# Attention, MLP and top-1 experts on one core: the expert memory taken from attention's rings, six of 13 late token slots turned by TensorE

## The chip, the cores and the metric

One core of a Trainium2 chip runs the whole program. The metric is the device time of one execution in microseconds (us), as the median of several runs. Engines are named as in the profile: PE is TensorE (PEld its weight loads), DVE is VectorE, ACT is ScalarE, POOL is GpSimd, SP is SyncE, which here only issues transfers. A tile pool with n buffers under one tag is called a ring: the n-th next user of the tag waits until the buffer's readers are done.

## The reference

Four batches of 8 heads, head width 64, with 512 local and 32 global tokens. Attention, then a plain MLP, then a mixture of eight experts of which each token takes one:

```python
s_ll = where(|i - j| <= 32, scale * q_l @ k_l.T, -1e9)       # local, window 32
a_l  = softmax(concat([scale * q_l @ k_g.T, s_ll]))
out  = concat([softmax(scale * q_g @ k_all.T) @ v_all, a_l @ v_all])
x    = out.reshape(2304, 512)
h    = x @ w_in                                              # 512 -> 2048
x    = (h * sigmoid(h)) @ w_out                              # 2048 -> 512
e    = argmax(x @ w_gate); p = softmax(x @ w_gate)[e]
out  = p * sigmoid(x @ w_output_gate)[e] * (relu(x @ w1[e]) @ w2[e])   # 512 -> 1024 -> 512
```

## The kernel before

Matrix products are made from 16-bit halves: each f32 operand is scaled by a power of two and split into a high and a low f16, and three products (high by high, high by low, low by high) are summed in PSUM. Batch 0's attention is in f32, so it can start on raw inputs.

**Start.** SP issues the loads in the order of the code (L1407 to L1417): q of tile 0, all of k of batch 0, cs (mask columns), q of tile 1, cr (a table of constants with the identity for PE's transposes), the first 1 MB of w_in, v of batch 0, and the rest. `scale_v0` (L315) squares v on ACT (L319), sums over partitions on PE (L192, `tot`) and derives the power-of-two scale of batch 0's v; then attention steps run: scores on PE (L475), softmax (L454), transposes of the probabilities on PE (L489, L490), products with v (L497, L498). DVE rebuilds f32 from the 64-bit w_in (L381 to L383). The instruction order on each engine is set by a scheduler that runs over the program before the launch; priorities (`tc.high_priority`, with URG = 2000 the most urgent) and `tc.issue_after` bend it.

**Middle.** The other attention steps are interleaved with the MLP: h products (L681), SiLU on ACT and DVE (L683 to L701), x products (L728). Each 128-token tile of x is split into halves x2s, which go to x2d in DRAM (L752, 512 columns high and 512 low).

**Routing.** x2f is turned on PE (x2t, L766) for the gate (L776). From one-hots come each token's rank in its expert and from that a slot of 128 tokens: 8 early slots, one per expert, filled from the first 15 tiles, and 23 others, of which 13 are worked on here ("late" slots). A product of A (position one-hots) with Rc or RE (slot one-hots) gives the row numbers: `pme` (L1124) and from it `idge` (L1125) for the early slots, `pm` (L1173) and from it `idg` (L1174) for the late ones. `pce` and `pcf` give the gate coefficients in the same way, `pt` the output rows.

**Experts.** Slot n's tokens are gathered from x2d by an indirect DMA on POOL (xg, L1241) and transposed by a DMA that SP issues (x, L1243). `mm_h` multiplies by a quarter (256 columns) of w1 (hp, L1286 or L1278 and L1281), makes relu and the halves on ACT and DVE (r, hb; L1299 to L1306), and has hb of two slots transposed by another DMA of SP (L1313). `mm_y` multiplies by the matching rows of w2 (yp, L1323) and adds into ys. Four such quarters ("chunks") run; weights come as 512 KB loads into the ring `ws` (L918) and are split by ACT (L954) and DVE (L955). w1 and w2 of chunk 0 are there before routing ends. The early slots run first, the late ones after `last()` (L1141), which makes idg. The buffers of the late part (`ys`, which also holds the gathered xg; `xs` for transposed x; `r` with three buffers for r and two for hb; six for ws) lie in pools that are opened when the routing's and the MLP's pools are closed:

```python
        rt_ctx.close()
        mlp_ctx.close()

        ys_p = ctx.enter_context(tc.tile_pool(name="ys", bufs=1))
        xs_p = ctx.enter_context(tc.tile_pool(name="xs", bufs=1))
        r_p = ctx.enter_context(tc.tile_pool(name="r", bufs=3))
        moe.pools = (xs_p, r_p, ys_p)
        wm["s"], wm["n"] = ctx.enter_context(tc.tile_pool(name="ws", bufs=6, side="right")), 3
```

Until then ws has two buffers. `rest` (L1352) then issues, in this order, the late gathers, chunk 0's coefficients and, behind the last late transpose, the loads of w1's next chunk.

Of the kernel before, what the change touches and what calls it, by code (L numbers as in the profile page):

```python
# [9 lines left out]
F32 = mybir.dt.float32  # L10
# [42 lines left out]
NEARLY = NE  # L53
ORDER = (*range(14), 16, 14, 15)
# [52 lines left out]
def tile_kernel(ctx: ExitStack, tc, csa, csr, q0, q, qn, qg, k0, k, va, vc, w_in, w_out, wg, w1, w2, out, dbg=None):  # L107
# [11 lines left out]
    g_p = mlp_ctx.enter_context(tc.tile_pool(name="g", bufs=6))  # L119
    gt_p = mlp_ctx.enter_context(tc.tile_pool(name="gt", bufs=2))  # L120
    x2_p = mlp_ctx.enter_context(tc.tile_pool(name="x2", bufs=2))
# [75 lines left out]
    woh = wto.tile([128, KF, DM], F16, name="woh")  # L197
    wol = wto.tile([128, KF, DM], F16, name="wol")
# [68 lines left out]
    def load_k0():  # L267
        kt[0] = k_p.tile([128, 4, S], F32, tag="k", name="k0")
        SP.dma_start(kt[0], k0)
# [35 lines left out]
    def load_v0():  # L305
        vt[0] = v_p.tile([128, 5, DM], F32, tag="v", name="v0")
        SP.dma_start(vt[0][:, 0:4], va[0])
        SP.dma_start(vt[0][0:SG, 4], vc[0])
# [136 lines left out]
    pt, av, sums, xs = {}, {}, {}, {}  # L445

# [5 lines left out]
    ident = cr[:, C_ID:C_ID + 128]  # L452

# [13 lines left out]
    def att0_s(t, pr):  # L467
# [4 lines left out]
        for hh in range(2):  # L472
            p, h = divmod(2 * pr + hh, 4)
            p = slice(64 * p, 64 * p + 64)
            PE.matmul(ps[:, hh, 0:wl], qt[t][p, h], kt[0][p, h, 128 * t:128 * t + wl])  # L475
            if t:
                PE.matmul(ps[:, hh, wl:wt], qt[t][p, h], kt[0][p, h, 0:SG])
        e = e_p.tile([128, 2, 256], F32, tag="e", name="e")
# [502 lines left out]
    def route(rt, rps):  # L981
# [9 lines left out]
        DVE.tensor_scalar(trib, iota, cr[:, C_P:C_P + 1], None, ALU.is_gt)  # L991
        ones = T([128, 128], "ones", BF16)
# [14 lines left out]
        Rc = T([128, NT, 3, NSLOT], "Rc", BF16)  # L1007
        Rce = Rc.rearrange("p i c n -> p (i c n)")[:, 0:45 * NEARLY].rearrange("p (i c n) -> p i c n", c=3, n=NEARLY)
        RE = Rce[:, :, 2]
# [26 lines left out]
        apend, pc_i = [], [None]  # L1036
# [55 lines left out]
        def early(i):  # L1092
# [11 lines left out]
            else:  # L1104
# [3 lines left out]
                coef(14, 15)  # L1108

                DVE.tensor_scalar(n0[:, 1], n0[:, 1], 128.0, None, ALU.max)  # L1110
                r, SR = slice(0, 15), [128, 15, NE]
                DVE.tensor_scalar(u[:, r, 0], dhi[:, r], 0.0, None, ALU.is_equal)
                DVE.tensor_tensor(RE, ohf[:, r], bc(u[:, r], SR), ALU.mult)
                static(0, 15)

        def early_slots():
            pump_a(99)
            SR = [128, 15, NEARLY]
            for c in range(2):
                DVE.tensor_tensor(Rce[:, :, c], RE, bc(row[c][:, 0:15], SR), ALU.mult)  # L1120
            pm = rps.tile([128, NEARLY], F32, tag="av", name="pme")
            for i in range(15):
                for c in range(2):
                    PE.matmul(pm, A[:, i], Rce[:, i, c], start=(i == 0 and c == 0), stop=(i == 14 and c == 1))  # L1124
            DVE.tensor_scalar(idge, pm, -1.0, 0.0, ALU.add, ALU.max)  # L1125
# [15 lines left out]
        def last():  # L1141
            p = onehot(15, 17)
            DVE.tensor_tensor(n0[:, 2], n0[:, 1], p[:, 0, 0], ALU.add)
            n1 = T([128, NE, 1], "n1")
            DVE.tensor_tensor(n1[:, :, 0], n0[:, 2], p[:, 0, 1], ALU.add)
            cmp = d.rearrange("p i e -> p (i e)").rearrange("p (e i) -> p e i", e=NE)
            S3t = [128, NE, NT]
            DVE.tensor_tensor(cmp, bc(n1, S3t), bc(cr[:, C_CNT:C_CNT + NT].rearrange("p (a i) -> p a i", a=1), S3t), ALU.is_gt)
            sl = T([128, NE], "sl")
            DVE.tensor_reduce(sl, cmp, AX.X, ALU.add)  # L1150
            DVE.tensor_scalar(sl, sl, -float(NS), 0.0, ALU.add, ALU.max)
            DVE.tensor_tensor_scan(bnd[:, 0], one8, sl, 0.0, ALU.mult, ALU.add)
            base = T([128, 1, NE], "base")
            DVE.scalar_tensor_tensor(base[:, 0], bnd[:, 0], float(ST - NS), sl, ALU.add, ALU.subtract)
            ranks(15, 17, p, n0[:, 1:3])
            static(15, 17)
            S3 = [128, NT, NE]
            DVE.tensor_tensor(tmp, ohf, bc(base, S3), ALU.mult)
            b_ = T([128, NT, 1], "b_")
            DVE.tensor_reduce(b_[:, :, 0], tmp, AX.X, ALU.add)  # L1160
            DVE.tensor_tensor(b_[:, :, 0], b_[:, :, 0], u[:, :, 0], ALU.mult)
            DVE.tensor_tensor(b_[:, :, 0], b_[:, :, 0], dhi, ALU.add)
            SR = [128, NT, NSLOT]
            R = Rc[:, :, 2]
            i24 = iota[:, 0:NSLOT].rearrange("p (a n) -> p a n", a=1)
            DVE.tensor_tensor(R, bc(i24, SR), bc(b_, SR), ALU.is_equal)
            for c in range(2):
                DVE.tensor_tensor(Rc[:, :, c], R, bc(row[c], SR), ALU.mult)
            pump_a(99)
            pm = rps.tile([128, NSLOT], F32, tag="av", name="pm")  # L1170
# [42 lines left out]
    class Moe:  # L1213
# [138 lines left out]
        def rest(self, ny, wq):  # L1352
            ne, ns = self.ne, self.ns
            self.experts()
            while wpend or wq:
                pump_w(wq)
# [233 lines left out]
```

## Time and profile before

| what | us |
|---|---|
| median of 3 runs (lowest, highest) | 865.5 (864.69, 870.08) |
| the profiled execution | 872.73 |
| span of its trace | 870.9 |
| mean granted TensorE clock | 0.964 of full speed |

The profile is of one execution. Its rows give the start in us from the span's beginning, the duration of a group of like instructions, engine, line, operation, output tile from input tiles, and in brackets how long the engine had stood idle before and what released it. Busy times per stretch are given per engine with the number of instructions; PEclk is the granted clock as a share of full speed, DMA the mean busy share of the core's 16 DMA engines.

### The profile page before, as it was taken

Reading aid. Unit: us, or ns where it says so; the run is one execution under the profiler, and the core shown is the slowest. Engines: PE = TensorE matmul, PEld = TensorE weight load, DVE = VectorE, ACT = ScalarE, POOL = GpSimd, SP = SyncE. Lnnn points to the kernel's source line nnn. Section 1 sums busy time; section 2 is a strip of 40 time slices with the busy share of each in tenths; the row PEclk is TensorE's granted clock in tenths of the full one; section 3 lists DMA queues with packets and bytes.
Section 4 is the critical chain, followed back from the end, with each engine's and each line's share of the span. In section 5 each row is a group of like instructions: output and inputs, shape, how many; then the busy total and the mean of one; then the engine's idle time right before and its main releaser. Section 6 shows DMA issues by size and latency. Waiting matters only on the chain.

```text
span 870.9 us, 17387 instructions
## 1 busy us (share of the span) xinstructions
PE 769.5 (88%) x6201; PEld 525.3 (60%) x6201; DVE 590.1 (68%) x1649; ACT 516.8 (59%) x1017; POOL 58.1 (7%) x110
## 2 busy tenths in 40 slices
PE   2999969899899999999999889968759998899894
PEld 2898656566666766677666557545425655455541
DVE  2978876777767878767565556872126787588862
ACT  2685768677667667666545555411359846756710
POOL 0000000000000000000000000035000000000054
PEclk9999888999999999999999999979979999999997
DMA  9733444366974284646354262199975974885672
GB/s 356 292 121 123 150 149 161 107 145 167 183 122 89 48 176 99 137 86 122 67 99 106 95 146 65 46 194 194 197 202 174 237 143 151 181 167 170 141 175 90
DMA packets 182139, 127.83 MB, mean 147 GB/s; under 512 B 161437, under 2 KB 162973, under 8 KB 178592
## 3 DMA queue, kind: packets, MB, share of 16 engines
q1 hardware_dynamic: 178688, 116.67, 55.5%
q0 software_dynamic: 3360, 9.97, 3.9%
q8 instruction: 54, 0.88, 0.4%
q14 instruction: 37, 0.30, 0.1%
HBM read 76.93 MB, written 9.96 MB: 100 GB/s over the span
## 4 chain that ended last, share of the span: by engine, by line
PE 42%; DMA 20%; DVE 14%; issue 9%; ACT 9%; SPq 2%; POOL 1%; POOLq 0%; ACTq 0%; DVEq 0%
PE h L681 10%; PE x L728 10%; DMA ws<-in_w_dram 6%; PE yp L1323 5%; DMA pT<-pb 4%; DMA wil<-hb 4%; PE hp L1286 3%; PE av L531 2%; PE s L475 2%; DMA st<-in_qn_dram 2%; DVE w1b L955 2%; DVE k L210 2%; PE av L497 1%; PE av L498 1%; ACT w1b L954 1%
## 5 line engine op out<-in xcount | busy, mean ns | idle before, releaser
L728 PE MATMUL x<-woh,g 128*128 128x512 f16 x544 | 173.5, 381 | 0.3 <-ACT g L711 0.3
L681 PE MATMUL h<-xT,wih 128*128 128x256 f16 (+1 forms) x1152 | 162.0, 272 | 3.6 <-DMA xT<-xb 1.5
L681 PEld LDWEIGHTS <-wih 128*128 128x128 f16 x1152 | 109.3, 100 | 29.5 <-issue 4.7
L728 PEld LDWEIGHTS <-g 128*128 128x128 f16 x816 | 76.3, 98 | 80.4 <-issue 2.6
L1323 PE MATMUL yp<-w2b,wil 128*128 (+1 forms) x384 | 93.4, 390 | 19.5 <-DMA wil<-hb 11.9
L728 PE MATMUL x<-wol,g 128*128 128x512 f16 x272 | 103.8, 382 | 0.0
L1286 PE MATMUL hp<-w1b,x 128*128 128x256 f16 (+1 forms) x672 | 87.8, 279 | 8.9 <-DMA x<-xg 4.7
L681 PE MATMUL h<-xT,wil 128*128 128x256 f16 (+1 forms) x576 | 87.3, 273 | 0.0
L1286 PEld LDWEIGHTS <-x 128*128 128x128 f16 x672 | 67.0, 101 | 27.6 <-issue 5.9
L464 ACT ACTIVATE e<-e,mx,esc 128x192 f32<-128x192 f32 (+1 forms) x128 | 70.5, 553 | 19.1 <-DVE mx L461 17.5
L228 ACT ACTIVATE junk<-ws 128x1024 f16<-128x1024 f32 x48 | 50.8, 1058 | 41.5 <-DMA ws<-in_w_dram 40.8
L1323 PEld LDWEIGHTS <-wil 128*128 128x128 f16 x384 | 38.0, 102 | 61.4 <-issue 13.4
L683 ACT ACTIVATE tanh<-h,th 128x512 f32<-128x512 f32 (+1 forms) x72 | 47.1, 658 | 41.9 <-PE h L681 41.7
L700 ACT ACTIVATE g<-tanh,i_out 128x512 f16<-128x512 f32 (+1 forms) x64 | 44.1, 692 | 33.8 <-DVE tanh L696 33.7
L681 PEld LDWEIGHTS <-wil 128*128 128x128 f16 x576 | 55.4, 100 | 7.2 <-issue 0.2
L701 DVE SCALAR_TENSOR_TENSOR g<-tanh,i_out,g 128x512 f16<-128x512 f32 (+1 forms) x64 | 45.7, 716 | 20.5 <-ACT g L700 20.3
L696 DVE SCALAR_TENSOR_TENSOR tanh<-tanh,h 128x512 f32<-128x512 f32 (+1 forms) x64 | 41.4, 649 | 26.6 <-ACT tanh L683 26.3
L460 DVE CUSTOM_DVE_ANT_0 e<-s,cs 128x192 f32<-128x192 f32 (+1 forms) x128 | 42.7, 370 | 19.7 <-PE s L450 11.0
L955 DVE SCALAR_TENSOR_TENSOR w1b<-ws,s,w1b 128x1024 f16<-128x1024 f32 x32 | 40.1, 1280 | 14.1 <-ACT w1b L954 14.0
L955 DVE SCALAR_TENSOR_TENSOR w2b<-ws,s,w2b 128x1024 f16<-128x1024 f32 x32 | 40.6, 1282 | 12.0 <-ACT w2b L954 9.5
L516 DVE SCALAR_TENSOR_TENSOR pb<-e,pb 128x384 f16<-128x384 f32 (+1 forms) x48 | 28.0, 587 | 18.6 <-ACT pb L515 18.2
L514 POOL MEMSET pb<- 128x256 f16 (+1 forms) x48 | 12.4, 259 | 360.9 <-DMA pT<-pb 144.6
(345 smaller groups left out, 1395.1 us busy)
## 6 DMA issues: line engine op xcount, KB each, us to landing
ws<-in_w_dram SPq DMA_DIRECT2D x64, 512.0 KB
st<-in_w_out_dram SPq DMA_DIRECT2D x8, 1024.0 KB
st<-in_w_in_dram SPq DMA_DIRECT2D x6, 1024.0 KB
q<-in_q_dram SPq DMA_DIRECT2D x12, 512.0 KB
x2d<-x2s SPq DMA_DIRECT2D x17, 256.0 KB
st<-in_k_dram SPq DMA_DIRECT2D x3, 1088.0 KB
st<-in_qn_dram SPq DMA_DIRECT2D x3, 1024.0 KB
st<-in_va_dram SPq DMA_DIRECT2D x3, 1024.0 KB
```

The costliest lines, as they stand in the source:

```text
L228: ACT.activation(junk, x, ACTF.Square, accum_out=m)
L460: DVE.tensor_tensor_reduce(dst[:, hh, 0:wt], ps[:, hh, 0:wt], mask, 1.0, -3e38, ALU.add, ALU.max, mx[:, hh:hh + 1])
L464: ACT.activation(dst[:, hh, 0:wt], dst[:, hh, 0:wt], ACTF.Exp, scale=esc[:, b:b + 1], bias=mx[:, 2 + hh:3 + hh], accum_out=sums[i][:, h:h ...
L681: PE.matmul(ps[:, f], w[:, kk, c], xj[:, l + kk, 0:n], start=(m == 0 and kk == 0), stop=(m == 2 and kk == KD - 1))
L683: pin[0] = ACT.activation(t, ps, ACTF.Tanh, scale=th[:, b:b + 1])
L696: pin[1] = DVE.scalar_tensor_tensor(t, t, 1.0, ps, ALU.add, ALU.mult)
L700: ACT.activation(hi, t, ACTF.Copy, scale=i)
L701: pin[2] = DVE.scalar_tensor_tensor(lo, t, i, hi, ALU.mult, ALU.subtract)
L728: PE.matmul(x2ps[2 * j + c], x[:, f, o], w[:, ff], start=(ff == 0 and m == 0), stop=(ff == KF - 1 and m == 2))
L955: DVE.scalar_tensor_tensor(d[:, 1], t[a], sc_, d[:, 0], ALU.mult, ALU.subtract)
L1286: PE.matmul(ps[:, 0], x[:, xl + kk], self.rows("1", n, l, kk), start=(m == 0 and kk == 0), stop=(m == 2 and kk == KD - 1))
L1323: PE.matmul(ps, h[:, hl + j], self.rows("2", n, l, j), start=(m == 0 and j == 0), stop=(m == 2 and j == KJ - 1))
```

## The change

Pools. woh and wol (w_out's halves) move from `wto` into `wts`, which stays to the end, and the MLP's rings xt, g, gt and x2 are no longer closed. The expert stage lives in them: late gathers and late results take `room(k, a)`, which is pairs of the xT ring for the first six late slots, then the x2 ring, and `ys` for three; transposed late x and the late hT take views of woh and wol (`xlate`); r takes the tanh ring (two buffers), hb and junk the g ring (six). ws has six buffers from the late MLP on.

Weights. w1's chunk 1 is prefetched before `moe.mm_h(0)`; the loops of `rest` are rewritten as one, with the same work per step.

Routing. `early_slots` and `last` run at the urgent priority and make the row numbers first; the coefficients and static tables are issued after them (`issue_after(key)`).

Turned slots. Late slots 1, 3, 5, 7, 9 and 11 (counted from the first late one) are transposed by PE into PSUM, eight 128x128 pieces with a 16-bit identity, and copied out by ACT or DVE.

Start. The loads are reordered and split, and v's scale is issued behind the scores of the fourth attention step. A branch of mm_y whose list of slots was empty is removed.

```diff
-    mlp_ctx = ExitStack()
-    wto = mlp_ctx.enter_context(tc.tile_pool(name="wto", bufs=1))
-    xt_p = mlp_ctx.enter_context(tc.tile_pool(name="xt", bufs=3))
...
+    xt_p = ctx.enter_context(tc.tile_pool(name="xt", bufs=3))
+    g_p = ctx.enter_context(tc.tile_pool(name="g", bufs=6))
+    gt_p = ctx.enter_context(tc.tile_pool(name="gt", bufs=2))
+    x2_p = ctx.enter_context(tc.tile_pool(name="x2", bufs=2))
...
+TURN = (1, 3, 5, 7, 9, 11)
...
+        def room(self, k, a):
+            if k < 6:
+                if k % 2 == 0:
+                    self.pair[a] = xt_p.tile([128, 2, DM], F32, tag="xT", name="yx")
+                return self.pair[a][:, k % 2]
+            if k < 10:
+                return x2_p.tile([128, DM], F32, tag=("x2s", "x2T")[k % 2], name="yx")
+            return self.ys_p.tile([128, DM], F32, tag=f"y{k}", name="yx")
...
         def gather_late(self, n):
...
+            k = n - self.ne
+            t, x, s = self.room(k, 0).bitcast(F16), self.xlate(k), self.slots[n]
+            if k not in TURN or not self.ne:
+                return self.gather(n, s, idg, NTOK, t, x)
+            self.x[n] = x
+            POOL.indirect_dma_start(out=t, out_offset=None, in_=x2d[0:NTOK, :],
+                                    in_offset=bass.IndirectOffsetOnAxis(ap=idg[:, s:s + 1], axis=0))
+            p = ps_x.tile([128, 2 * KD, 128], F16, tag="x2", name="xt16")
+            for j in range(2 * KD):
+                PE.transpose(p[:, j], t[:, 128 * j:128 * j + 128], id16)
+            if k % 4 == 1:
+                ACT.activation(x, p, ACTF.Copy)
+            else:
+                DVE.tensor_copy(x, p)
...
-                r = self.pools[1].tile([128, CH], F32, tag="r", name="r")
-                    self.hb[q] = self.pools[1].tile([128, 2, 2, CH], F16, tag="hb", name="hb", bufs=2)
+            r = gt_p.tile([128, CH], F32, tag="tanh", name="r")
+                self.hb[q] = g_p.tile([128, 2, 2, CH], F16, tag="g", name="hb")
...
+        def early_slots():
+            SR = [128, 15, NEARLY]
+            with tc.high_priority(URG):
+                pump_a(99)
...
+                key_i[0] = DVE.tensor_scalar(idge, pm, -1.0, 0.0, ALU.add, ALU.max)
+            with tc.issue_after(key_i[0].ins):
+                DVE.tensor_scalar(n0[:, 1], n0[:, 1], 128.0, None, ALU.max)
+                coef(14, 15)
                 static(0, 15)
...
         load_q(0)
+        SP.dma_start(cs[:, 0:WT[0]], csa[:, 0:WT[0]])
         load_k0()
-        SP.dma_start(cs, csa)
+        load_w(("i", 0))
+        SP.dma_start(cr, csr)
+        load_v0()
+        load_w(("i", 1))
         load_q(1)
-        SP.dma_start(cr, csr)
-        load_w(("i", 0))
-        load_v0()
+        SP.dma_start(cs[:, WT[0]:], csa[:, WT[0]:])
+        load_v0_rest()
...
-        scale_v0()
         while npos[0] < P["n0"]:
             att_step()
+            if npos[0] == 4:
+                with tc.issue_after(sc0[0].ins):
+                    scale_v0()
...
-                    wm["s"], wm["n"] = rt_ctx.enter_context(tc.tile_pool(name="ws", bufs=2, side="right")), 1
+                    wm["s"], wm["n"] = ctx.enter_context(tc.tile_pool(name="ws", bufs=6, side="right")), 3
...
+        wq1 = [(1, "1", p) for p in range(4)]
+        prefetch(wq1)
         moe.mm_h(0)
...
-        mlp_ctx.close()
```

What moves on the engines is shown at three places. First SP's queue at the start of the program; q is a query tile, st, wil and wih hold parts of w_in. Before:

```order
L256 DMA q_166<-in_q_dram 128x512
L269 DMA k_168<-in_k_dram 128x2176
L1408 DMA cs<-in_csa_dram 128x608
L256 DMA q_171<-in_q_dram 128x512
L1410 DMA cr<-in_csr_dram 128x590
L375 DMA st<-in_w_in_dram 128x1024
L307 DMA v_176<-in_va_dram 128x2048
L308 DMA v_176<-in_vc_dram 32x512
```

The same queue now:

```order
L256 DMA q_167<-in_q_dram 128x512
L1427 DMA cs<-in_csa_dram 128x192
L270 DMA k_170<-in_k_dram 128x1088 x2
L379 DMA st<-in_w_in_dram 128x1024
L1430 DMA cr<-in_csr_dram 128x590
L308 DMA v_176<-in_va_dram 128x1024
L379 DMA st<-in_w_in_dram 128x1024
L256 DMA q_180<-in_q_dram 128x512
L1434 DMA cs<-in_csa_dram 128x416
L311 DMA v_176<-in_va_dram 128x1024
```

k is loaded in two halves, most of cs, the second q and half of v stand behind two parts of w_in. On PE the first matmul was the sum over v's squares (L192); now eight score products, eight transposes and twelve products with v stand ahead of it.

Second, SP's queue where the MLP ends and the experts begin: L1243 (L1260 now) transposes gathered x, L1313 (L1344 now) hidden halves, L918 (L925 now) loads weights. Before:

```order
L1313 DMA_TRANSPOSE wil<-hb 128x8x128
L1243 DMA_TRANSPOSE x<-xg 128x8x128
L1313 DMA_TRANSPOSE wil<-hb 128x8x128 x3
L1243 DMA_TRANSPOSE x<-xg 128x8x128 x13
L918 DMA ws<-in_w_dram 128x1024 x6
L1313 DMA_TRANSPOSE wil<-hb 128x8x128 x4
L1313 DMA_TRANSPOSE hT<-hb 128x8x128 x2
L1313 DMA_TRANSPOSE hT<-hb 128x4x128
```

Now:

```order
L925 DMA ws<-in_w_dram 128x1024 x2
L759 DMA x2d<-x2s 128x1024
L1260 DMA_TRANSPOSE x<-xg 128x8x128 x8
L759 DMA x2d<-x2s 128x1024 x2
L1344 DMA_TRANSPOSE wil<-hb 128x8x128 x3
L1260 DMA_TRANSPOSE woh<-yx 128x8x128
L1344 DMA_TRANSPOSE wil<-hb 128x8x128
L1260 DMA_TRANSPOSE woh<-yx 128x8x128
L1560 TENSOR_LOAD eidx
L1560 ISA x2
L1260 DMA_TRANSPOSE woh<-yx 128x8x128 x2
L1260 DMA_TRANSPOSE wol<-yx 128x8x128 x3
```

The eight early transposes stand in one row ahead of the last two writes of x2d, the late ones are seven instead of 13, and the six weight loads that stood behind them are earlier in the queue.

Third, DVE where idge is made (Rc and ohs hold one-hots, x2f is a copy of the MLP's last output, tanh and g are SiLU's tiles, u, rk, cf and cp tables of the routing). Before:

```order
L1069 CAST cp<-cf 128x1
L763 COPY x2f<-x_7161 128x512
L742 TENSOR_REDUCE tm<-x_7161 128x1
L1089 TENSOR_TENSOR rk<-rk,u 128x15
L1071 TENSOR_TENSOR cf<-cf,cp 128x1
L742 TENSOR_REDUCE tm<-x_7162 128x1
L1127 TENSOR_TENSOR Rc<-Rc,cp 128x15x8
L1090 SCALAR_TENSOR_TENSOR dhi<-rk,dhi 128x15
L1069 CAST cp<-cf 128x1
L1125 TENSOR_SCALAR idge<-pme 128x8
```

Now:

```order
L1118 TENSOR_SCALAR u<-dhi 128x15
L1119 TENSOR_TENSOR ohb<-ohf,u 128x120
L1126 TENSOR_TENSOR ohs<-ohb,cr 128x15x8 x2
L703 SCALAR_TENSOR_TENSOR tanh<-tanh,h 128x512
L708 SCALAR_TENSOR_TENSOR g<-tanh,i_out,g 128x512
L1131 TENSOR_SCALAR idge<-pme 128x8
L1133 TENSOR_SCALAR n_5949<-n_5949 128x8
L1065 TENSOR_TENSOR d<-lg,mx 128x8
```

idge stood behind the copy of the last x and among the coefficient steps; it now stands between the SiLU steps of the last MLP group, and the coefficient steps follow it. On PE, the 30 pme matmuls that were behind the last x product are now ahead of 35 h and 60 x products.

## Rows read from the trace of the kernel before

**Rows 1.** The page: busy time, share of the span and instructions
```profile
PE 769.5 (88%) x6201; PEld 525.3 (60%) x6201; DVE 590.1 (68%) x1649; ACT 516.8 (59%) x1017; POOL 58.1 (7%) x110
```

**Rows 2.** Busy per stretch: length, PE PEld DVE ACT POOL, PEclk, DMA share, GB/s
```profile
0.00:17.40 17.40, 0.55 (x3) 0.54 (x3) 3.14 (x3) 3.89 (x4) 0.47 (x10) 1.00 0.92 338
17.40:77.70 60.30, 59.87 (x240) 53.53 (x240) 51.79 (x139) 41.73 (x105) 0.10 (x1) 1.00 0.58 216
...
132.00:462.00 330.00, 318.08 (x3282) 220.81 (x3275) 239.98 (x702) 221.10 (x463) 13.79 (x55) 0.99 0.57 120
462.00:565.70 103.70, 97.53 (x799) 65.13 (x797) 65.99 (x202) 58.48 (x92) 0.00 (x0) 0.98 0.34 93
565.70:643.00 77.30, 49.59 (x383) 32.37 (x380) 27.03 (x128) 21.05 (x44) 20.92 (x21) 0.85 1.02 211
...
700.00:858.00 158.00, 142.51 (x860) 83.72 (x859) 115.74 (x267) 87.09 (x157) 17.84 (x17) 0.99 0.65 159
```

**Rows 3.** Timeline of the start, and of the first h product
```profile
11.34 0.69 DVE L381 TENSOR_SCALAR woh<-st 128x1024 int32<-128x1024 int32 x1 [11.34 <-DMA st<-in_w_in_dram]
...
14.79 1.91 ACT L319 ACTIVATE junk<-v 128x2048 f16<-128x2048 f32 x1 [12.77 <-DMA v<-in_va_dram]
...
16.85 0.58 PE L192 MATMUL tot<-vm,cr 128*128 128x1 f32 x2 [16.85 <-ACT junk L319]
...
77.66 0.42 PE L681 MATMUL h<-xT,wih 128*128 128x256 f16 x1
```

**Rows 4.** DMA rate in 40 slices of 1.5 us, 0 to 60 us
```profile
GB/s 0 213 409 382 402 445 431 437 332 270 365 415 415 431 431 426 410 421 392 357 426 426 385 74 109 437 164 0 0 5 0 55 295 350 262 388 310 89 0 0
```

**Rows 5.** Timeline of DVE in the transition
```profile
564.25 0.69 DVE L763 COPY x2f<-x 128x512 f32<-128x512 f32 x1
...
566.75 0.15 DVE L1125 TENSOR_SCALAR idge<-pme 128x8 int32<-128x8 f32 x1
...
586.34 0.18 DVE L1174 TENSOR_SCALAR idg<-pm 128x31 int32<-128x31 f32 x1
```

**Rows 6.** Timeline of POOL and of SP's DMA issues in the transition
```profile
593.99 0.95 POOL L1241 DMA_INDIRECT xg<-x2d,idg  x1 [10.66 <-DVE hb L1305]
...
589.57 1.29 SPq L1243 DMA_TRANSPOSE x<-xg  x1
...
602.76 26.93 SPq L1243 DMA_TRANSPOSE x<-xg  x13
629.86 3.26 SPq L918 DMA_DIRECT2D ws<-in_w_dram  x6
```

**Rows 7.** Timeline of PE in the transition
```profile
563.62 0.38 PE L728 MATMUL x<-wol,g 128*128 128x512 f16 x1
563.84 0.81 PE L728 MATMUL x<-woh,g 128*128 128x512 f16 x3
...
565.67 1.07 PE L766 MATMUL x2t<-cr,x2f 128*128 128x128 f32 x8
...
643.05 3.57 PE L1323 MATMUL yp<-w2b,wil 128*128 x8 [10.46 <-DMA wil<-hb]
```

**Rows 8.** DMA queues: 602 to 630 (two rows), then 593 to 634
```profile
q1 hardware_dynamic: 12946, 3.22, 76.3%
q0 software_dynamic: 708, 2.31, 36.4%
...
q0 software_dynamic: 1040, 3.41, 33.9%
```

**Rows 9.** A late slot's r, its expert product, and the page's weight conversion
```profile
615.15 0.39 ACT L1299 ACTIVATE r<-hp 128x256 f32<-128x256 f32 x1
...
616.48 0.42 DVE L1302 SCALAR_TENSOR_TENSOR hb<-r,hb 128x256 f16<-128x256 f32 x1 [0.48 <-ACT hb L1301]
...
650.14 1.47 PE L1286 MATMUL hp<-w1b,x 128*128 x12
...
L955 DVE SCALAR_TENSOR_TENSOR w1b<-ws,s,w1b 128x1024 f16<-128x1024 f32 x32 | 40.1, 1280 | 14.1 <-ACT w1b L954 14.0
```

More of the change, by code (lines that the diff above doesn't have):

```diff
@@ L1159, in last @@
[L1159 to L1168, printed above, removed]
@@ L1169, in last @@
-            pump_a(99)
-            pm = rps.tile([128, NSLOT], F32, tag="av", name="pm")
-            for i in range(NT):
-                for c in range(2):
-                    pm_i = PE.matmul(pm, A[:, i], Rc[:, i, c], start=(i == 0 and c == 0), stop=(i == NT - 1 and c == 1))
-            DVE.tensor_scalar(idg, pm, -1.0, 0.0, ALU.add, ALU.max)
-            for c in range(2):
-                DVE.tensor_tensor(Rc[:, :, c], R, bc(row[2 + c], SR), ALU.mult)
-            pm = rps.tile([128, NSLOT], F32, tag="av", name="pt")
@@ L1216, in __init__ @@
             self.ev, self.x, self.hT, self.ys, self.hb, self.cc = {}, {}, {}, {}, {}, {}
-            self.pools, self.xg = None, []
+            self.late, self.xg, self.pair = False, [], [None, None]
             for n, x in enumerate(slots):
@@ L1274, in mm_h @@
             ps = p.tile([128, 2, CH], F32, tag=tag, name="hp")
-            wide = bool(self.pools) and (n % P["wm"]) in P["wide" if n < ST and self.ne else "dwide"]
+            wide = self.late and (n % P["wm"]) in P["wide" if n < ST and self.ne else "dwide"]
             if wide:
@@ L1324, in mm_y @@
                               start=(m == 0 and j == 0), stop=(m == 2 and j == KJ - 1))
[L1325 to L1329 removed]
+            if c == 0:
                 if n < self.ne:
@@ new lines, in rest @@
+                for kd in ("1", "2"):
+                    busy = c > 0 or kd == "2"
+                    for n in [n for n in self.order if c or n >= (ne if kd == "1" else ny)] + [None]:
+                        if n is not None:
+                            if kd == "1":
+                                self.mm_h(n)
+                            else:
+                                self.mm_y(c, n)
+                        while busy:
+                            if wpend or cur:
+                                pump_w(cur, P["KS"])
+                            else:
+                                busy = False
+                                if kd == "1":
+                                    self.coefs(c)
+                                cur = [(c + 1, "21"[kd == "1"], p) for p in range(4)] if c + 1 < NCH else []
+                                prefetch(cur)
+                            if n is not None:
+                                break
@@ L1539, in tile_kernel @@
             moe = Moe(list(range(NMAIN, NSLOT)), 0)
-            moe.pools = (xs_p, r_p, ys_p)
-            moe.rest(0, [(0, kd, p) for kd in ("1", "2") for p in range(4)])
+            moe.ys_p, moe.late = ys_p, True
+            wq = [(0, kd, p) for kd in ("1", "2") for p in range(4)]
+            while wpend or wq:
+                pump_w(wq)
+            moe.rest(0, [(1, "1", p) for p in range(4)])
 def prep(q_l, k_l, v_l, q_g, k_g, v_g, moe_w_in, moe_w_out, moe2_w_gate, moe2_w_output_gate, moe2_w1, moe2_w2):
```

241 lines of the change are left out of this document (111 added, 130 removed).

## The prediction, made before the run

> **What bounds the kernel now.** I first read the busy times of the page [rows 1]: PE works 769.5 of 870.9 us, so 101 us at most can come out of its idle time, and no other engine is over 68%. An average does not say where those 101 us lie, so the next view is the table of busy times by stretch [rows 2], cut at the points where the work changes kind. PE is busy 0.55 us of the first 17.40, 59.87 of 60.30 in the attention behind it, 318 of 330 in the middle of the MLP, 49.59 of the 77.30 in which MLP turns into experts, and 142.5 of 158 in the last chunks. Two stretches hold some 44 us of idle PE: 16.9 at the start and 27.7 in the transition. The rest of it lies thin.
>
> At the start the timeline [rows 3] says who ends the wait. PE's first matmul (16.85) is the sum over v's squares, released by an ACT pass over v that waited for v's transfer until 14.79. The scores of batch 0 need q0, k0 and part of cs, which are first in SP's queue, but stand behind that sum on PE. DVE first works at 11.34, when the first part of w_in lands.
>
> In the transition the DMA engines are full: 1.02 of their time [rows 2]. The last MLP output leaves PE at about 565.7 (T0 from here). The row numbers that say where the late slots' tokens lie (idg) are out at 586.34 [rows 5], T0+20.6, but the first late gather starts only at 593.99, after a DVE write of hb at the end of the early experts [rows 6]: the late buffers lie in pools that open when the MLP's have closed. 13 gathers follow, then 13 transposes (602.76 to 629.7 on SP), behind them six 512 KB weight loads, and then hb's transposes. PE's late matmuls wait for all of it, the last time 10.46 us, until 643.05 [rows 7]. So here the end is set by the data path gather, transpose, hidden transpose, not by PE.
>
> **The change part by part.**
>
> *Start.* SP issues the same bytes in another order, and PE gets eight scores in front of the sum. When do they land? Before w_in's first MB stand 3.30 MB in the queue (q0 0.26, k0 1.11, cs 0.31, q1 0.26, cr 0.30 and itself 1.05). It landed at 11.34, when the rates of the 1.5 us slices [rows 4] sum to 3.79 MB; so 0.49 MB of later transfers had come as well. With the same 0.49 MB added, the new order gives: q0, 192 columns of cs and half of k0 (0.92 MB) at 5.7 us; all of k0 (1.47) at 7.2; w_in's first (2.52) at 9.5; cr with the identity (2.83) at 10.3; half of v (3.35) at 11.5; w_in's second (4.40) at 14.6. PE could thus begin about 10 us earlier (17.36 to about 7), and hold part of it while cr and v come. DVE begins 5.4 us earlier (11.34 to about 6), and then waits some 2.5 us for cr and w_in. PE's 59.87 us of 60.30 say that PE is the tighter one of the two; DVE has 8.5 us of slack there. So the gain lies between DVE's 5.4 - 2.5 = 3 us and the whole distance of 12 (16.85 - 5.7, and one for the smaller start of DVE). I take 9, near PE's row, since PE's is the fuller engine. The scale of v moves behind four attention steps; what hides it is that PE's order has eight transposes and twelve products of probabilities and v before that sum now, so nothing on PE is kept by it. Without that cover it would cost the wait for v again, up to the 9. q1 and the rest of v come at about 15 and 16 us and are first used after eight score products. From 77.66 on PE has so little idle time (12 of 330) that the shift is carried to the end.
>
> *Transition, early slots.* idge and its chain are now ahead of the last x products. Before, it came out at 566.75, T0+1.1 [rows 5], and the last of the eight early transposes was issued at 589.57, T0+23.9 [rows 6]. Now the 30 pme matmuls stand ahead of 35 h and 60 x products. An x matmul starts every 0.22 us [rows 7], one of 256 columns every 0.12 [rows 9], so idge comes some 60 x 0.22 + 35 x 0.12 = 17 us before T0; the gathers then lie beside MLP matmuls, with the DMA engines at 0.34 there [rows 2].
>
> *Transition, late slots.* Five edits act together. (a) With the buffers in attention's rings the gathers wait for idg, no longer for hb: idg at about T0+17.5 (three us earlier, as the static coefficients are issued behind it), gathers from T0+18 instead of T0+28.3. (b) Six of 13 transposes leave the DMA engines. In 602 to 630 the hardware queue took 76.3% of 28 us for the 13, so 1.64 us each, and in 593 to 634 the 13 gathers took 33.9% of 41 us, 1.07 each [rows 8]. Now 13 x 1.07 + 7 x 1.64 = 25.4 us instead of 35.2, beside hidden transposes. (c) The six weight loads, 512 KB each, are issued before the transition, not behind the transposes; they land beside MLP matmuls, where the DMA engines have room. (d) PE gets 48 more matmuls, 128x128 in 16 bits. No row shows one. From above: eight f32 transposes took 1.07 us [rows 7], 0.134 each, 6.4 us. From below: half of a 256-column product (12 in 1.47 us [rows 9]), 0.06 each, 2.9 us. I take 4, between them. (e) Their six copies out of PSUM, three on ACT and three on DVE, are 1024 wide; the nearest row is a 512-wide f32 copy of 0.69 us [rows 5], so 0.7 to 1.4 us each. Beside DVE's 27 and ACT's 21 us of work in 77.3 they hide; without cover they cost at most 8 us.
>
> The new length by two ways. By data: gathers from T0+18, 25.4 us of DMA time plus the hidden transposes among it end around T0+45 to 50, and the last hidden transpose and its landing follow, some 8 to 10: late y starts at T0+53 to 60. By PE: 49.6 us of work, less about 5 of it that came at a granted clock of 0.85 [rows 2], plus 4, gives 49. The data path is the later one, so late y starts near T0+58 instead of T0+77.3: 19 us. Bounds: 28 if PE's 49 decides, 8 if only the DMA time of the six transposes goes (6 x 1.64 = 10) and PE pays some of it back.
>
> The row says 1.64 us for a transpose of 256 KB. The Trainium skill (Advanced Engine Details and Errata, DMA Advanced Topics, X-Bar Transpose) states that transposing DMAs are as fast as regular ones, at 350 to 400 GB/s, which is about 0.7 us each, an estimate from that page; the six would then give back 4 us and not 10, and the sum would be some 6 us higher. The trace contradicts it here. For the PE side, the skill (TensorE: Matmul & The Clock Gate, Part 4: PE-mode transpose) gives about 275 ns for one in a kernel, which would be 13 us for 48, an estimate from that page, and speaks against the change; the f32 row at 0.134 us bounds it lower.
>
> *Late chunks.* r now has two buffers (it shares the tanh ring) instead of three, hb six instead of two. For a slot r is written by ACT and last read by DVE 1.75 us later (615.15 to 616.90), and a slot comes every 1.3 us or more [rows 9]. Two buffers last 2.6 us, so a slot may be late by 0.85 us before PE waits; the cover is that slack. I cost it at nothing, and its failure is a rival. The weight ring is six in both. The cost of the dead branch removed is nothing.
>
> *Sum.* 9 + 19 = 28 off 872.7 (the profiled execution, span 870.9) gives 844.7. That execution is 7.2 us above the median of the runs, 865.5, so the forecast is 865.5 - 28 = 837.5.
>
> **The rivals.**
> B: *the DMA engines stay the bound.* They were at 1.02 [rows 2], and the loads that move ahead only fill the time before. The transition then gives only the six transposes, 10, and the start 9: 865.5 - 19 = 846.5. For it speaks that gathers and hidden transposes remain; against it that idg had lain ready for 7.5 us when the first late gather went, and that wait goes.
> C: *both pay in full:* 11 at the start, 28 in the transition, PE's floor: 826.5.
> D: *little of either:* the start gives 2, as DVE takes PE's place as the bound there (51.79 of 60.30), and the transition 5: 858.5.
> E: *slower, by the r ring.* In chunks 1 to 3 there are 63 slots. DVE converts weights in pieces of 1.28 us [rows 9]; a slot whose DVE step falls behind one is late by half of it, 0.64, on the mean, and by the whole if two pieces meet. Where lateness passes 0.85 us, PE stops with the ring. If every slot paid the 0.64, it would be 40 us: 865.5 - 28 + 40 = 877.5. Against it: PE is idle only 15.5 us of these 158 with DVE at 73% [rows 2], and only some slots meet a conversion.
>
> **How the numbers follow.** The forecast (A, its own range 828 to 847) 0.55, B 0.20, C 0.12, D 0.07, E 0.06. About 1% (8.7 us) is what a measurement of this kernel can tell from no change, so the borders are 856.8 and 874.2. Faster: A, B and C, 0.87; within: D, 0.07; slower: E, 0.06. The range that leaves out the outer part of C and D and all of E is 822 to 856.
>
> **What would show it.** At the start: first PE work at about 7 us, a score product, and the first h product at about 69 instead of 77.66. In the transition: early gathers before the last x product, first late gather within 1 us of idg, seven transposes of x behind it, 16 or so PE transposes per pair of slots at under 0.14 us, and late y about 58 us behind the last x. In the late chunks: waits of PE or ACT on r under 5 us in sum. It is wrong if PE's first h product has not moved, if the late x's transposes still end 60 us behind T0, or if the 158 us of the late chunks grow by more than 5.

## The result, and the profile after

The changed kernel takes 836.1 us (median of 4 runs, 833.9 to 836.5); the kernel before took 865.1 in the same comparison. The ratio is 0.9648, with a 95% interval of 0.9612 to 0.9683. The forecast was 837.5. The kernel before was timed again beside each experiment below, with medians of 865.8 to 870.7, so the ratios compare better than the times; they leave out executions over 1.5% longer than the fastest of their kernel.

The total agrees, but it is a sum of terms, so the first thing to look at is the same table as in [rows 2], now of the changed kernel, cut at the points that answer to the old ones: first PE work, first h product, the end of the last x product (T0), the first late y product, the end. Columns: length, busy time of PE, PEld, DVE, ACT and POOL, granted clock, DMA share, GB/s.

```profile
0.00:7.30 7.30, 0.00 (x0) 0.02 (x1) 0.00 (x0) 1.28 (x1) 0.65 (x12) 1.00 0.71 225
7.30:69.10 61.80, 61.79 (x240) 57.06 (x241) 52.40 (x141) 41.63 (x101) 0.10 (x1) 1.00 0.81 278
69.10:122.10 53.00, 39.58 (x301) 31.70 (x298) 46.76 (x101) 34.00 (x69) 0.62 (x2) 0.89 0.43 119
122.10:560.50 438.40, 418.14 (x4090) 287.18 (x4091) 310.02 (x918) 285.64 (x573) 21.16 (x61) 0.99 0.57 129
560.50:617.50 57.00, 48.76 (x451) 35.57 (x450) 35.88 (x149) 21.76 (x46) 12.91 (x13) 0.97 0.85 166
617.50:834.00 216.50, 191.15 (x1175) 115.89 (x1173) 155.38 (x347) 133.41 (x233) 21.39 (x21) 0.96 0.63 163
```

The old profile's execution lay 7 us above the median of its runs, so a second one of the kernel before (867.2 us, E0 below) is the better partner. The same table of it:

```profile
0.00:16.20 16.20, 0.01 (x1) 0.01 (x1) 3.14 (x3) 3.35 (x4) 0.47 (x10) 1.00 0.91 333
16.20:77.00 60.80, 60.37 (x241) 54.00 (x242) 51.79 (x139) 42.16 (x105) 0.10 (x1) 1.00 0.60 220
77.00:130.00 53.00, 43.82 (x318) 34.67 (x320) 45.92 (x110) 36.38 (x75) 0.62 (x2) 0.88 0.42 138
130.00:563.60 433.60, 417.09 (x4053) 286.41 (x4046) 305.47 (x901) 278.50 (x553) 13.75 (x55) 0.99 0.51 113
563.60:639.40 75.80, 49.76 (x409) 33.53 (x406) 27.59 (x131) 21.64 (x44) 20.61 (x21) 0.80 1.02 215
639.40:865.40 226.00, 196.06 (x1196) 116.58 (x1196) 155.65 (x367) 134.03 (x240) 22.17 (x21) 0.98 0.65 161
```

Read from top to bottom: the first h product comes 7.9 us earlier (77.0 to 69.1), the last x product ends only 3.1 us earlier (563.6 to 560.5), the transition is 18.8 us shorter (75.8 to 57.0), and the rest 9.5 (226.0 to 216.5). In the rest the old kernel still has the hidden products of two late slots, 20 matmuls or some 2.5 us by [rows 9], that the changed one has done by then, so 7 of the 9.5 are a gain of the late chunks. The sum is 31.4 between these two executions and 29 between the medians. So the transition came out as forecast, most of the start's lead was gone by the last x product, and the late chunks made up for it.

The timeline rows that answer to [rows 5 to 7] (columns as there):

```profile
543.77 0.17 DVE L1131 TENSOR_SCALAR idge<-pme 128x8 int32<-128x8 f32 x1 [1.08 <-PE pme L1130]
...
576.15 0.19 DVE L1188 TENSOR_SCALAR idg<-pm 128x31 int32<-128x31 f32 x1
...
576.61 0.94 POOL L1258 DMA_INDIRECT yx<-x2d,idg  x1 [17.90 <-DVE idg L1188]
...
601.62 1.06 PE L1291 MATMUL xt<-id,yx 128*128 128x128 f16 x16
...
617.55 2.75 PE L1354 MATMUL yp<-w2b,wil 128*128 x12
```

The early key idge now precedes T0 by 16.7 us, the late key idg comes at T0+15.6, the first late gather 0.3 us behind it, and the first late y at T0+57.0. A run of sixteen PE transposes takes 1.06 us, 0.066 each and 3.2 us for 48; one by itself lasts 0.22 in the record, but they overlap.

### The profile page after: what moved, and what is told of

Same layout as the page of the kernel before. It is cut to its first block, busy times and chain, and to the rows that moved or that the text cites. A ratio compares the mean times of both kernels' runs of the same rounds, so it can differ in the third digit from the quotient of the medians.

```text
span 834.0 us, 17487 instructions
## 1 busy us (share of the span) xinstructions
PE 759.4 (91%) x6249; PEld 527.4 (63%) x6249; DVE 600.4 (72%) x1653; ACT 517.7 (62%) x1020; POOL 56.8 (7%) x110
## 4 chain that ended last, share of the span: by engine, by line
PE 41%; DMA 12%; DVE 7%; ACT 5%; issue 3%; SPq 1%; POOLq 0%; ACTq 0%; DVEq 0%
PE h L688 9%; PE x L735 9%; PE yp L1354 9%; PE hp L1325 6%; DMA ws<-in_w_dram 5%; DMA pT<-pb 4%; PE hp L1317 2%; PE av L538 2%; DMA wil<-hb 1%; DVE w1b L962 1%; ACT w1b L961 1%; DMA woh<-yx 1%; PE hp L1320 1%; ACT junk L228 1%; ACT w2b L961 1%
## 5 line engine op out<-in xcount | busy, mean ns | idle before, releaser
L1325 PE MATMUL hp<-w1b,x 128*128 128x256 f16 x384 | 48.7, 279 | 1.2 <-ACT r L1338 1.2
L1325 PEld LDWEIGHTS <-x 128*128 128x128 f16 x384 | 38.6, 102 | 10.7 <-issue 2.1
L1364 DVE SCALAR_TENSOR_TENSOR yx<-yp,cc,yx 128x512 f32<-128x512 f32 x39 | 29.1, 748 | 8.9 <-PE yp L1354 8.8
```

Of the source, the lines that this page charges most:

```text
L1325: PE.matmul(ps[:, 0], x[:, xl + kk], self.rows("1", n, l, kk), start=(m == 0 and kk == 0), stop=(m == 2 and kk == KD - 1))
```

## The experiments

In the stage numbers below, T0 is the end of the last x product, "transition" the way from T0 to the first late y product, "rest" what follows to the end of the span.

**E0, the kernel before again.** Edit: none.

> The kernel before once more, for a second profile: its first one (872.7 us) lay 7 us above the median of its runs. Between the two profiles, from the first late y product on, the changed kernel is 11.4 us shorter (227.9 against 216.5), for which the forecast had nothing. Theory: most of those 11.4 belong to that one execution, so this profile comes near 865 us with the same start (first PE work near 17, first h product near 77.7) and a transition of 77 us, and the stretch from the first late y product to the end is 220 to 223. Rival: the late chunks really are 10 us shorter with the change, and the 7 us lie in the transition, which then takes 70 us here.

Measured: 867.2 us, span 865.4. T0 563.6, transition 75.8, rest 226.0 (in the first profile 565.1, 78.0 and 227.9). The theory is wrong: the 5.5 us between the two profiles are spread over all stages, some two in each, and the rest is 226.0, not 220 to 223. The rival is right that the late chunks really are shorter with the change, and wrong about a transition of 70.

**E1, the old start in the changed kernel.** Edit: the order of loads and scale_v0 as before.

```diff
-        SP.dma_start(cs[:, 0:WT[0]], csa[:, 0:WT[0]])
         load_k0()
-        load_w(("i", 0))
...
+        scale_v0()
         while npos[0] < P["n0"]:
```

> The changed kernel with the old order of loads and the scale of v back in front. Theory: the start's gain (8.5 us at the first h product) is partly lost in the middle (5.3 are left at the last x product), so the time rises by 5 to 8.5, to 841 to 845 us, with first PE work near 17 and the first h product near 77.5. Rival: the middle of the MLP is bound by something that does not start earlier, so the gain is lost on the way and the time rises by 2 at most, to 836 to 838.

Measured: 845.1 us, ratio to the kernel before 0.978 (0.968 to 0.987). The first h product comes at 76.6, but T0 is at 560.7, as in the changed kernel (560.5). One profile does not tell T0 to better than some 5 us: E3, E8 and E9 below, which differ from the changed kernel only behind T0, have it at 556.3, 561.2 and 558.9. So at the last x product the start is worth between nothing and some 4 us. The transition is 64.8 instead of 57.0, with one wait of 12 us in it:

```profile
591.70 0.19 DVE L1195 TENSOR_SCALAR oh<-pt 128x31 f32<-128x31 f32 x1 [10.22 <-remote]
...
593.59 2.72 PE L1350 MATMUL yp<-w2b,wil 128*128 128x512 f16 x6 [12.05 <-ACT wih L1358]
```

DVE waits 10.2 us for the product pt, of which PE's records show the last matmul at 581.5; "remote" means that no recorded instruction ended the wait. The time falls in the theory's range, then, for another reason: of the 9 us more in this profile 7.8 lie in the transition that holds this wait. That the wait makes them is argued; no run has the old start without it.

**E2, the new start alone in the kernel before.** Edit: E1's, the other way round.

> The kernel before with only the new start. Theory: 5 to 8.5 us less than before, 857 to 860, first h product near 69, the transition unchanged at 77 us. Rival: 862 to 865, the gain at the first h product being lost before the last x product.

Measured: 866.1 us, ratio 0.9975 (0.993 to 1.002), no change. The first h product comes at 69.6, T0 at 562.7, 0.9 us before E0's. The rival holds: the lead is lost before the last x product. Part of the loss is in PE's waits. Its two longest behind the first h product are here

```profile
120.33 1.13 PE L572 MATMUL s<-k,qgs 64*32 64x272 f32 x8 [5.57 <-DVE tb L180]
...
126.26 1.03 PE L687 MATMUL h<-xT,wih 128*128 128x256 f16 x4 [4.49 <-DMA xT<-xb]
```

and in E0

```profile
120.94 1.00 PE L566 MATMUL s<-k,qgs 64*32 64x272 f32 x8 [2.69 <-DVE tb L180]
...
128.13 1.01 PE L192 MATMUL tot<-qm,cr 128*128 128x2 f32 x4 [2.05 <-ACT ge L574]
```

The score products s that end the first wait start at nearly the same time in both. The wait for xT has no counterpart in E0. Another part belongs to this execution. Behind 0.7 us of idle PE at 88.8 us the granted clock falls to 0.50 (1.2 instead of 2.4 GHz) for 91 to 97 us; the changed kernel has the same idle time at 88.2 and keeps 1.00. E2 comes out of this stretch 3.2 us further behind the changed kernel.

**E3, no turned slots.** Edit: `TURN = ()`.

> The changed kernel with all 13 late slots transposed by DMA. Theory (the data path ends the transition): six more transposes of 1.64 us on full DMA engines, less 3.2 us that PE spends on its transposes: 5 to 9 us longer, 841 to 845, with the first late y product 5 to 10 us later behind the last x product than 57. Rival (PE is the floor, 48.9 of 57.1 us busy there): the DMA time hides beside PE's work and PE gains 3 us, 833 to 836.

Measured: 835.5 us, ratio 0.965 (0.953 to 0.977), the same as with turned slots. Its profile has T0 at 556.3, a transition of 61.5 with the same unnamed wait as E1 (10.3 us), and a rest of 213.5. The time is in the rival's range, the first late y product 4.5 us later, near the theory's. Whether the wait hides a gain is for E8 and E9.

**E5, the early key late.** Edit: the early slots' row numbers and gathers are issued behind the MLP's last product and without the urgent priority, and their coefficients ahead of them; the weight ring keeps six buffers.

```diff
                         early(16)
-                        early_slots()
-                        moe = Moe(...)
-                        for n_ in range(NEARLY):
-                            moe.gather_early(n_)
...
+        early_slots()
+        moe = Moe(...)
+        for n_ in range(NEARLY):
+            moe.gather_early(n_)
         while wpend or wq:
```

> The changed kernel with the early slots' row numbers, tables and gathers issued after the MLP's last product, as before. Theory (most of the transition's 19 us come from the early gathers, which now lie beside MLP products): idge comes about 2 us behind the last x product instead of 17 us ahead of it, the first early product about 8 us later, and the first late y product 66 to 72 us behind the last x product instead of 57: 844 to 851 us. Rival (the gain comes from the late gathers, which no longer wait for hb and closed pools): at most 3 us more, 836 to 839.

Measured: 852.8 us, ratio 0.985 (0.981 to 0.990): 16.7 us more than the changed kernel. idge comes 2 us behind T0, the transition is 79.4, longer than the theory's 66 to 72, and the rest 212.1. Its rows: idge, POOL's last early and first late gather, and PE's waits in the transition (in all, times, longest):

```profile
562.26 0.15 DVE L1134 TENSOR_SCALAR idge<-pme 128x8 int32<-128x8 f32 x1
...
579.64 1.05 POOL L1257 DMA_INDIRECT xg<-x2d,idge  x1 [1.76 <-DVE hb L1338]
582.11 1.35 POOL L1257 DMA_INDIRECT yx<-x2d,idg  x1 [1.41 <-issue]
```

```profile
PE hp L1324 <- DMA x<-xg: 13.3, 4, 7.4
PE yp L1353 <- DMA wil<-hb: 9.6, 2, 6.8
```

The late gathers start at T0+21.8, some 7 us ahead of E0's T0+29.4, six slots are turned by PE, the weight loads lie earlier, and the transition is still 3.6 us longer than before. So without the early key nothing of that stage's gain is left.

**E6, the weight ring of two.** Edit: ws as before, two buffers until the routing's pools close; chunk 1's loads behind that.

```diff
-                    wm["s"], wm["n"] = ctx.enter_context(tc.tile_pool(name="ws", bufs=6, side="right")), 3
+                    wm["s"], wm["n"] = rt_ctx.enter_context(tc.tile_pool(name="ws", bufs=2, side="right")), 1
```

> The changed kernel with the weight ring ws of two buffers until the routing's pools close, as before, and w1's chunk 1 loaded behind that; the key-first order of the routing and all else stay. In the kernel before, the rank product pc stood behind a weight statistic (tot) in PE's order, since both take the same PSUM ring, and tot waits for weights that come through two buffers: pc ran at 548.4 of 563.6 us (last x product), in the changed kernel at 515.9 of 560.5. Theory (the weight ring made the early key late, so it carries the transition's gain): idge comes 1 to 3 us behind the last x product again, the first late y product 74 to 80 us behind it, 848 to 855 us. Rival (the order key first, coefficients later is what moved the key): idge stays 15 us or more ahead, 836 to 841 us.

Measured: 853.1 us, ratio 0.980 (0.973 to 0.987); idge 1.4 us behind T0, transition 78.1, all in the theory's ranges. Why a ring of weights holds a table of the routing is seen in PE's timeline of this run:

```profile
539.70 0.38 PE L192 MATMUL tot<-mw,cr 128*128 128x2 f32 x2
539.95 0.21 PE L1040 MATMUL pc<-ohb,ones 128*128 128x112 bf16 x1
...
555.13 0.90 PE L1130 MATMUL pme<-ohs,A 128*128 128x8 bf16 x30
```

The statistic tot of w2's last pieces and the rank product pc take buffers of one PSUM ring (`av`), and pc is issued behind tot; tot comes in steps of some 12 us here (502.7, 515.0, 527.7, 539.7), as weights pass through two buffers. In the changed kernel, with six, no tot stands between 500 us and T0, and pc runs at 515.9. E5 shows that the late key is enough for such a transition; what chunk 1's later loads add to this run is not told apart.

**E10, the key first in the kernel before.** Edit: the routing's new order and priority in the old kernel, ring of two.

> The kernel before with the early key first, at the urgent priority, and its coefficients and tables behind it; the weight ring keeps two buffers. Theory: without the larger ring the key hardly moves (idge at most 3 us earlier against the last x product) and the time stays within 4 us of the kernel before, 861 to 867 us. Rival: the order alone brings the early gathers beside the MLP, 848 to 856 us.

Measured: 872.6 us, ratio 1.004 (1.001 to 1.008): over the theory's 861 to 867, but within its 4 us of the kernel before, which took 870.7 beside it. tot and pc stand late again, and idge is 1.4 us behind the last x product:

```profile
547.18 0.38 PE L192 MATMUL tot<-mw,cr 128*128 128x2 f32 x2
547.42 0.21 PE L1031 MATMUL pc<-ohb,ones 128*128 128x112 bf16 x1
...
564.15 0.15 DVE L1122 TENSOR_SCALAR idge<-pme 128x8 int32<-128x8 f32 x1
```

The order of the key gains nothing without the ring. Nor does the ring without the order: in E5, with six buffers, pc runs at 516.4 and idge still comes behind T0. The early key needs both.

**E7, r and hb swap rings.** Edit: in the late chunks r takes the ring of six, hb that of two.

> The changed kernel with the two rings swapped in the late chunks: r takes the ring of six, hb the ring of two (before: three and two). Theory (late chunks became shorter since hb has six buffers, and two for r are enough): PE's waits on r rise from 3 us towards the 6 us that they were before, 838 to 842 us. Rival 1: hb's ring is not the cause, 834 to 838. Rival 2 (the forecast's rival E): r's two buffers do cost something, so this kernel is faster, under 834.

Measured: median 840.1 us of runs from 836.1 to 859.3, ratio 0.968 (0.963 to 0.972). The median is in the theory's range, but the interval overlaps the changed kernel's, so neither the theory nor rival 1 is decided; and the profiled execution is the longest, 859.3 us, so its waits are not set against the changed kernel's. Rival 2 falls: faster than the changed kernel it is not, so two buffers for r cost nothing that this can see, unless hb's two cost here what r's six give. How much of the late chunks' gain is hb's ring stays open.

**E8 and E9, the registers read early.** Edit: the experts' numbers (eidx) are computed, and read into PE's registers, ahead of idg; E9 also has no turned slots.

```diff
+                DVE.tensor_copy(eidx[:, ND:ND + 1], bnd[:, 0, NE - 1:NE])
+                moe.experts()
                 ranks(15, 17, p, n0[:, 1:3])
```

> The changed kernel with the experts' numbers computed, and read into PE's registers, ahead of idg, that is before the late gathers start. In the kernel before and in three experiments PE's result came 2 to 10 us late to DVE or ACT at the place where PE reads its registers while gathers run; the changed kernel's profile shows no such wait. Theory: nothing to gain here, idg about 1 us later, 834 to 838 us. Rival: the late result has another cause and appears here by chance, 842 to 848.

> The same, with all 13 late slots transposed by DMA. Theory (the unnamed 10 us wait of the kernel without turned slots hangs on the register reads beside the gathers): the wait is gone and the time falls from 835.5 to 823 to 830 us. Rival: the wait is still there, 833 to 838.

Measured: E8 837.6 us (0.968; 0.963 to 0.973), E9 837.1 us (0.968; 0.963 to 0.973). Neither has an unnamed wait. E8 is as its theory says; E9's, 823 to 830, is wrong: the wait is gone and the time stays. The transitions are 59.2 and 64.6, the rests 215.4 and 210.2: in these two profiles turning six slots is worth 5 us until the first late y, and the late chunks give them back. So the unnamed wait had hidden nothing in E3: that kernel's transition is 61.5 with the wait and E9's 64.6 without it. PE's waits in the rest name a part of what takes the 5 us back, in the changed kernel:

```profile
PE yp L1354 <- ACT w2b L961: 5.3, 2, 2.7
```

and in E3:

```profile
PE yp L1354 <- DVE w2b L962: 0.5, 1, 0.5
```

PE reaches w2 of the next chunk before ACT has converted it. In E8 and E9 the same wait is 2.7 us and 0.9, and that for hidden transposes 5.7 and 3.8; the rest of the 5 us is not named.

**E11, the transpose ahead of the loads.** Edit: at E2's second wait (in the changed kernel 4.9 us at 122.95), SP issues attention's transposed tile xT ahead of batch 1's q and k, 2 MB, instead of behind them. For that the end of attention tile 3 moves ahead of the next step's scores, at the urgent priority, and q and k come 2.5 to 3.7 us later.

```diff
+        if n == 16:
+            st_v(pairs[15])
+            with tc.high_priority(URG):
+                att_e(3)
...
-            load_qk(1)
+            with tc.issue_after(xb1[-1].ins):
+                load_qk(1)
```

> The changed kernel with one thing moved: the transpose of attention tile 3 (xT) is issued by SP ahead of the loads of batch 1's q and k (2 MB) instead of behind them. There PE waited 4.9 us for that transpose, which took 7.8 us from issue to landing beside the loads. Theory (part of the start's lead is lost here): the transpose lands some 4 us earlier, the h product at 122.95 comes at 118 to 120, and 1 to 4 us of that reach the end: 832 to 835 us. Rival (DVE's weight conversions and the later q and k take it back): 835 to 838 us.

The place in the changed kernel, SP's issues and PE's next two waits:

```profile
112.74 0.33 SPq L274 DMA_DIRECT2D st<-in_qn_dram  x1
114.47 0.33 SPq L276 DMA_DIRECT2D st<-in_k_dram  x1
115.17 1.98 SPq L668 DMA_TRANSPOSE xT<-xb  x1
```

```profile
116.58 1.13 PE L573 MATMUL s<-k,qgs 64*32 64x272 f32 x8 [5.25 <-DVE tb L180]
...
122.95 1.03 PE L688 MATMUL h<-xT,wih 128*128 128x256 f16 x4 [4.93 <-DMA xT<-xb]
```

and in E11:

```profile
116.51 1.13 PE L573 MATMUL s<-k,qgs 64*32 64x272 f32 x8 [5.30 <-DVE tb L180]
118.19 1.03 PE L688 MATMUL h<-xT,wih 128*128 128x256 f16 x4 [0.25 <-DMA xT<-xb]
```

Measured: the wait is gone, the h product comes 4.8 us earlier, and T0 is at 550.1, 10 us ahead of the changed kernel's profile and 6 ahead of E3's. The time is 837.2 us, ratio 0.9645 (0.959 to 0.971): not faster, in the rival's range, though not by the rival's cause, since T0 keeps what the edit won. The profile has the unnamed wait again:

```profile
581.12 0.19 DVE L1204 TENSOR_SCALAR oh<-pt 128x31 f32<-128x31 f32 x1 [9.80 <-remote]
```

**E12, both.** Edit: E11 with E8's early register reads.

> The kernel of the last experiment (xT ahead of batch 1's loads) with the experts' numbers read into PE's registers ahead of idg, as in the experiment on the register reads. Theory: the 9.8 us late result that the profile of the one had goes, while its earlier last x product (550 instead of 560 us) stays in part: 826 to 832 us, that is 0.955 to 0.96 of the kernel before. Rival: what comes earlier is taken back by the late chunks' weight conversion, as without turned slots: 833 to 838 us, 0.963 to 0.97.

Measured: 826.1 us (823.8 to 830.0), ratio 0.954 (0.949 to 0.958), as its theory says and below the changed kernel's interval. The profile has no unnamed wait; its stages:

```profile
69.50:552.40 482.90, 455.70 (x4390) 319.41 (x4389) 357.90 (x1017) 318.87 (x641) 21.91 (x63) 0.98 0.55 130
552.40:611.60 59.20, 50.45 (x451) 36.32 (x450) 34.97 (x149) 21.49 (x46) 12.95 (x13) 0.94 0.92 162
611.60:822.80 211.20, 189.85 (x1175) 114.90 (x1173) 155.62 (x347) 133.33 (x233) 21.97 (x21) 0.97 0.66 167
```

T0 (552.4) stays early, and the transition is that of E8. Against E8, which differs from it in E11's edit alone, the ratio falls from 0.968 to 0.954. T0 is 11.2 us ahead of E0's, more than the 7.5 of the first h product, so E11's edit does not only keep the start's lead; what it would give with the old start was not run. Against E11's profile the transition is 4.4 us shorter and the rest 6.0, while T0 is 2.3 later: more than the unnamed wait has changed.

## Why the prediction was right, and where it was not

**Start, 9 us: wrong at the end of the stage.** The way to the first h product was right: first PE work at 7.3 (forecast about 7), first h at 69.1 (forecast about 69). The step that failed is "From 77.66 on PE has so little idle time (12 of 330) that the shift is carried to the end". The row it rests on begins at 132; between 77.7 and 132 lies a stretch that the forecast's table left out. PE is busy 43.8 of 53.0 us there in E0 and 39.6 in the changed kernel, which waits more, with w_out's conversions and batch 1's loads beside it, and those start hardly earlier: batch 1's q is issued at 112.7 instead of 114.4. But the lead does not go there alone. Followed by SP's writes of x2d, one per token tile, it is 3.1 us at the second (181.2 against E0's 184.3), 7.9 again at the seventh (347.5 against 355.4) and 2.6 at the ninth (405.1 against 407.6). Between the seventh and the ninth PE waits 2.5 us, until 359.4, for a transposed pT, and the granted clock is 0.50 for some 3 us behind that; E3, with a wait of 0.8 us there and no such fall, still leads by 6.8 at the ninth. Few idle microseconds in an average did not mean that nothing would wait once the work came earlier. E11 shows one such transfer, a transpose behind 2 MB of loads; which others there are stays open. Measured value of the term: 0 to 4 us at T0 (E1 against four profiles with the new start), and by E2's time 2 us, with an interval of -2 to 6.

**Early key, transition: right in size, wrong in cause.** 18.8 us against 19, first late y at T0+57 against about T0+58. idge was forecast 17 us ahead of T0 and came 16.7 ahead. But the working put the gain down to five edits of the late slots, and E5 leaves all five in place with no gain at all: they are worth something only behind an early key. With the early slots late, their 13.3 us of waits for x hold PE, whatever the late gathers do. And what moved the key is not priority and order alone, as the forecast took for granted with "idge and its chain are now ahead": without the larger weight ring they do not move it (E6, E10), nor does the ring without them (E5). The prediction named that ring only as "The weight ring is six in both", which holds for the late chunks, but not for the end of the MLP, where it was two before.

**Turned slots: 10 us of DMA time, 5 at the first late y, none at the end** (E3; E8 against E9). The 1.64 us per transpose is an upper bound: the two queues' shares in [rows 8] add up to 113%, so their packets' times overlap. PE's transposes cost 3.2 us, near the 4 taken. The Trainium skill (TensorE: Matmul & The Clock Gate, Part 4: PE-mode transpose) gives about 275 ns for one in a kernel. The trace's 0.22 us for one is near that, but it is not the price of each in a run, where 16 took 1.06 us.

**Late chunks, 0: wrong by some 7 us.** "I cost it at nothing" held for r's two buffers: PE's waits on r fell from 5.8 us (E0's rest) to 2.9, where rival E had them grow. What was not priced is that the other edits help there: waits on y's sums go from 4.5 us to none. Waits for converted w2 take back most of this (0.8 to 6.3), and of the 7 us 4.6 are idle time of PE and 2.4 busy time. Which edit gives them is not shown; E7 leaves open whether hb's ring has a part in it.

**Rivals.** B (DMA stays the bound) fell with a transition of 57 us and DMA at 0.85 of its time there. C fell: neither term paid in full. D had the start's size at T0, but not its cause (the first h product did come 7.9 us earlier, so DVE did not hold it up), and was wrong about the transition. E fell. The forecast's 28 and the measured 29 agree since some 5 to 9 us missing at the start and 7 unforeseen ones at the end cancel. That is luck, and the total alone would have taught nothing of this.

## What to carry to other kernels

A lead won at one place counts only at the next stage that was waiting for it: follow it through every stretch, above all the one that the table leaves out, and look for the transfer that queues behind loads that nobody needs yet. When a small, urgent table is late, look for what shares its ring of PSUM or its queue: here the routing's own order brought nothing until the weights had six buffers, and without either the changed kernel loses 17 us. And do not take a total that fits for terms that fit.

## What the runs showed of the hardware

A result of PE came late, with no recorded instruction that ended the wait, in the stretch where gathers and transposes fill the DMA engines: 2.2 us in the first profile of before, 7.8 in E0, 10.2, 8.1 and 10.3 in E1 to E3, 8.0 (and 7.5 just before it) in E6, 8.7 in E10 and 9.8 in E11; none in the changed kernel, E5 and E7. In the three runs that read the experts' numbers into PE's registers before the gathers start (E8, E9, E12) the wait is absent, and between E11 and E12, which differ in that alone, the ratio falls from 0.9645 to 0.954. That the reads cause the wait is not shown. In E1, E3 and E11 they stand still in the middle of it; but in E6 the wait is over at 599.3, before the first read at 599.6, and in E0 and E10 the last read is done 7 and 10 us before the wait begins. What PE did in E6's wait is in the record: it ran one to three matmuls at a time, these 0.7 to 1.7 us apart, and before each it stood idle with nothing that the profile shows to wait for ("issue"). Some of them:

```profile
589.06 0.18 PE L1196 MATMUL pt<-wil,A 128*128 128x31 bf16 x1 [0.47 <-issue]
590.47 0.23 PE L1196 MATMUL pt<-wil,A 128*128 128x31 bf16 x2 [1.23 <-issue]
...
596.16 0.40 PE L1325 MATMUL hp<-w1b,x 128*128 128x256 f16 x1 [0.32 <-issue]
596.85 0.37 PE L1325 MATMUL hp<-w1b,x 128*128 128x256 f16 x1 [0.29 <-issue]
```

So it is PE that comes late there, not its result alone; why it does stays open.
